# Linear attention followed by a feed-forward layer: loads in batch order with waits between, a second pair of batches worked batch by batch, and a re-tuned order

## The chip, the cores and the metric

The kernel runs on one core of a Trainium2 chip. The metric is the device time of one execution in microseconds (us), smaller is better. Before the change the median of three runs was 384.72 us (383.87 to 385.67). All runs compared below are fast runs, that is, runs not disturbed by the slower state that some executions show.

The engines are called by their names in the profile: PE is TensorE (PEld its weight loads), DVE is VectorE, ACT is ScalarE, POOL is GpSimd, SP is SyncE. SyncE computes nothing; it issues transfers, and its records in the timeline carry the name SPq.

## The reference

There are 8 batches, 8 heads, 576 tokens, a head size of 64 and 128 features. Attention is linear, and its result is the input of a layer norm and a feed-forward layer of 512 to 2048 to 512 columns.

```python
def phi(x):
    proj = np.einsum('bhsd,df->bhsf', x, w_phi)
    proj = proj - np.max(np.abs(proj), axis=-1, keepdims=True)
    return np.concatenate([np.exp(proj), np.exp(-proj)], axis=-1)
q_p, k_p = (phi(q), phi(k))
kv = np.einsum('bhsf,bhsd->bhfd', k_p, v)
z = np.sum(k_p, axis=2)
num = np.einsum('bhsf,bhfd->bhsd', q_p, kv)
den = np.einsum('bhsf,bhf->bhs', q_p, z)[..., None] + 1e-06
attn = num / den                       # then heads side by side: x, (8, 576, 512)
# feed-forward
xn = (x - mu) / np.sqrt(var + 1e-06) * g_ln
out = x + np.maximum(xn @ w_ch1, 0.0) @ w_ch2
```

## The kernel before

The work is cut into 32 units. A unit is two heads: in the first pair of batches two heads of the same batch, in the later pairs one head of each of the two batches. A unit passes through all engines. TensorE transposes q and k (units 0 to 7; from unit 8 on transposing transfers do it), projects them (`pk`, `pq`, `pt`), and makes kv (`n_bank`) and the numerators (`num`). VectorE takes maxima, ScalarE exponentials, GpSimd scales v (`vv`) and writes the tokens (`x`).

When all eight heads of a batch are done, its tokens are complete. Then feed-forward blocks can run: `hT` (input times w1) and `ch` (times w2). Until the first of them, fillers, which are products of zeros (`wz`), are there to keep TensorE's clock up.

A small list scheduler decides the order of the instructions at build time. It plays the program through with estimated durations; on each engine it takes the ready operation with the smallest rank. The rank is the latest start plus a tuned offset, `OFF`, by stage and table. The order it finds is then fixed: on the chip every engine works through its own line in order.

```python
BLOCKS = (((0, 2), (2, 4), (4, 6), (6, 9)), *(((0, 3), (3, 6), (6, 9)),) * (NPAIR - 1))
...
def heads(pair, i, half):
    if pair == 0:                       # first pair: batch by batch
        return i // 4, 2 * (i % 4) + half, 2
    return 2 * pair + half, i, 1        # later pairs: one head of both batches
...
def stage_table(n):                     # three tables of offsets for 32 units
    return (n >= H // 2) + (n >= H)
...
for i in range(EXB):
    ex = consts.tile([P, 2, 2 * P], BF16, name=f"ex{i}")
    nc.gpsimd.memset(ex, 0.0)           # five of them, on GpSimd
...
load_weights()
for n in range(NW):
    load_w1(n, -5 + n, [("came", "q", 1)])
for key in "kqv":
    load_tails(key, 4, next(rank), "SP")
for n in (4, 5):
    for key in "kvq":
        load_main(key, n, 1, next(rank), "SP")
for n in range(NW):
    load_w2(n, rk("w2", 0))             # w2 waits only for w1
```

Of the kernel before, what the change touches and what calls it, by code (L numbers as in the profile page):

```python
# [17 lines left out]
def bcast(ap: bass.AP, dim: int, n: int) -> bass.AP:  # L18
# [9 lines left out]
OFF = (  # L28
    {
        "en": 0, "gln": 404.4, "k": 731.6, "k.copy": 69.4, "k.em": -232.2, "k.exp": 2503.5,  # L30
        "k.max": 95, "k.trans": 40.9, "kv": 899.6, "kv.copy": -103, "ln": 482.7, "mixed": 18.6,
        "mixed.exp": -123.6, "mixed.max": 174.2, "num0": -2477.8, "num0.dve": -58.1,
        "num0.put": 178.6, "num1": 209.2, "num1.dve": 318.7, "num1.put": -457.6, "q.copy": -276.1,
        "q.trans": -426.8, "q0": -1263.9, "q0.em": 149.7, "q0.max": 0, "q1": -821.5,
        "q1.em": -990.6, "q1.max": -13.6, "tails0": -719.9, "tails0.exp": -90.7, "tails1": -225.7,
        "tails1.exp": 0, "vv": 215.8, "w2": 3061.6, "x.copy": -132.9, "x.trans": -1573.1,
    },
    {
        "en": 1225.8, "k": -596.1, "k.copy": 123.9, "k.em": 639.7, "k.exp": 9.2, "k.max": 81.3,
        "k.trans": -90.1, "kv": 0, "kv.copy": -360, "ln": 262.7, "load": 0, "mixed": -1206,  # L40
        "mixed.exp": -223.1, "mixed.max": 1308.1, "num0": 517.5, "num0.dve": -73.3,
        "num0.put": 141.8, "num1": 67.4, "num1.dve": -802.1, "num1.put": 0, "q.copy": -784.4,
        "q.em": 5.6, "q.max": 36.6, "q.trans": 753.5, "qt": -360.9, "rstd": -179.5,
        "tails.exp": 199, "vv": 2452.3, "x.copy": 195.6, "x.trans": -942.9,
    },
    {
        "en": 167.8, "k": 108.9, "k.em": 424.2, "k.exp": -788, "k.max": 25.2, "kv": -30.9,
        "kv.copy": 8.3, "ln": 12.2, "load": 1357.4, "mixed": -2096, "mixed.exp": 54.6,
        "mixed.max": 4.8, "num0": -162.6, "num0.dve": -161.9, "num0.put": -15.2, "num1": -692.4,
        "num1.dve": -457.5, "num1.put": -223.9, "q.em": -210.7, "q.max": -16.1, "qt": -860.5,  # L50
        "rstd": 81.2, "tails.exp": -53.9, "trans": 253.4, "vv": 2822.4, "w1": 1149.9,
    },
)
# [9 lines left out]
class Order:  # L63

    ENGINES = ("PE", "DVE", "ACT", "POOL", "SP")
    START, LAND, RING, TURN, COLD = 1.15, 0.75, 60.0, 0.095, 5.5
# [36 lines left out]
    def run(self):  # L103
# [21 lines left out]
        while True:  # L125
# [30 lines left out]
            for engine in self.ENGINES:  # L156
# [4 lines left out]
                while queue:  # L161
                    item = heapq.heappop(queue)
                    op = item[2]
                    if op.engine:
                        op = None
                        continue
                    full = op.dma and out.get(op.dma[0], 0.0) > self.RING
                    if not full and all(room[res] >= n for res, n in op.acquire):
                        break
                    passed.append(item)  # L170
                    op = None
                for item in passed:
                    heapq.heappush(queue, item)
# [13 lines left out]
                if engine == "PE":  # L187
                    us += self.TURN * (op.mode != mode) + us * (now < self.COLD)
                    mode = op.mode
                elif engine == "DVE" and op.port:  # L190
                    us += min(max(free["POOL"] - now, 0.0), 1.0)
# [7 lines left out]
                if op.dma:  # L199
                    out[op.dma[0]] = out.get(op.dma[0], 0.0) + op.dma[1]  # L200
                    push(now + self.START, 3, op)
# [12 lines left out]
def kernel(  # L214
# [44 lines left out]
    EARLY, NUMB, TILED = 4, 0, 4  # L259
# [13 lines left out]

    wphi_f = consts.tile([P, F], FP32, name="wphi_f")
# [12 lines left out]
    for i in range(2):  # L287
        rows = slice(i * D, (i + 1) * D)
        nc.vector.tensor_copy(out=wbk[rows, i, :], in_=wphi_f[rows, :])
# [24 lines left out]
    for i in range(EXB):  # L314
        ex = consts.tile([P, 2, 2 * P], BF16, name=f"ex{i}")
        nc.gpsimd.memset(ex, 0.0)
        ex_bufs.append(ex)

    w1_sb = consts.tile([P, KC, DH], BF16, name="w1")
    w2_sb = consts.tile([P, JC, DM], BF16, name="w2")  # L320

# [9 lines left out]
    nc.vector.tensor_copy(out=wst, in_=wphi_f)  # L331
# [30 lines left out]
    def issue(queue, rank, dst, src, keys, nbytes, row=1024):  # L362
        eng = nc.sync if queue == "SP" else nc.scalar
        dma(
            queue, rank, nbytes / row, lambda: eng.dma_start(out=dst, in_=src), w=keys,
            us=0.65 if row == 256 else 0.52, ns=0.019 if row == 256 else 0.045,
        )

    def heads(pair, i, half):

        if pair == 0:
            return i // 4, 2 * (i % 4) + half, 2
        return 2 * pair + half, i, 1

    def load_main(key, n, nu, rank, queue):
# [7 lines left out]
        if pair == 0:  # L383
# [9 lines left out]
                262144 * nu,  # L393
            )
            return
        for half in range(2):
# [7 lines left out]
                [(key + str(half), g % NBUF, u) for u in us], 131072 * nu,  # L404
            )

    def load_tails(key, n, rank, queue):
# [4 lines left out]
        for half in range(2):  # L412
# [9 lines left out]
            issue(queue, rank, dst, src, [(key + "x" + str(half), j)], 16384 * TG, row=256)  # L422
# [25 lines left out]
    def load_w2(n, V):  # L448
# [9 lines left out]
        dma("POOL", V, 512, emit, r=[("w1 came", NW - 1)], w=[("w2", n)], us=0.75, ns=0.094)  # L458

    def scale_w1(n, rank):  # L460
# [5 lines left out]
        def scale(kc):  # L466
            nc.vector.tensor_scalar(
                out=w1_sb[:, kc, sl], in0=w1_sb[:, kc, sl], scalar1=gln_sb[:, kc : kc + 1],
                scalar2=-1.0, op0=ALU.mult, op1=ALU.mult,
            )  # L470

        for kc in range(KC):
            add("DVE", 0.3, rank, lambda kc=kc: scale(kc), r=["gln"], w=[("w1", n, kc)])
# [63 lines left out]
    def a_trans_dma(u):  # L537
# [28 lines left out]
        def turn():  # L566
# [6 lines left out]
        add(("DVE", "ACT", "POOL"), (0.12, 0.19, 0.8), rank, cast_mixed,  # L573
# [5 lines left out]
            us=1.3, ns=0.019)  # L579

    def a_mixed(u):
# [11 lines left out]
        def maxima():  # L593
            nc.vector.reduce_max(
                out=u["m"][:, :, u["mx"]],
# [28 lines left out]
    def a_k(u):  # L624
# [17 lines left out]
        def em():  # L642
            t_ = u["em", 1]
            e = u["mx"] + 1
# [7 lines left out]
        def en():  # L652
            e = u["mx"] + 1
            nc.scalar.activation(u["en"][:, 0:e], u["m"][:, 1, 0:e], AF.Exp, scale=-1.0)

        def scale_main(t):
            vb, vx = v_bufs[u["g"] % NBUF], vx_bufs[n // TG % 2]
# [5 lines left out]
            )  # L663
            nc.gpsimd.tensor_copy(  # L664
# [5 lines left out]
                in1=bcast(bcast(e[:, u["mx"] : u["mx"] + 1], 1, 2), 3, D1), op=ALU.mult,  # L670
# [14 lines left out]
        for t, e in ((1, ("em", 1, n % NEM)), (0, ("en", n % NEM))):  # L685
            add("POOL", 1.5, rk("vv", n), lambda t=t: scale_main(t),
                r=[e, *vdata] + [("vv", 1, n % VVB)] * (1 - t), w=[("vv", t, n % VVB)])

    def q_part(u, s):

        qT = u["qkT"][:, 0:512]
        if s is None:
            return qT.rearrange("p (c t) -> p c t", t=P)
        return qT.rearrange("p (h s t) -> p s h t", h=2, s=2)[:, s]

    def a_q(u, s=None):

        n = u["n"]
        x = "" if s is None else str(s)
        nc_ = 4 if s is None else 2  # L700

        def products():
            shape = [P, 2 * nc_, F]
            pool, tag = (ps_A, "A") if s is None else (ps_B, "B")
            u["pq", s] = ps = pool.tile(shape, FP32, tag=tag, name="pq")
            chunks = q_part(u, s)
            for c in range(nc_):
# [4 lines left out]
        def maxima():  # L712
            m, ps = u["m"][:, 0, :], u["pq", s]
            if s is not None:
                out = m[:, 6 * s : 6 * s + 4]
            elif u["pair"]:
                out = m[:, 0:MX]
            else:
                out = m.rearrange("p (s r) -> p s r", s=2)[:, :, 0:4].rearrange(
                    "p s (h a) -> p h s a", h=2  # L720
                )
                ps = ps.rearrange("p (h s a) f -> p h s a f", h=2, s=2)
            nc.vector.reduce_max(out=out, in_=ps, axis=AX.X, apply_absolute_value=True)

        def em():
            lo, hi = {None: (0, u["mx"] + 1), 0: (0, 4), 1: (6, u["mx"] + 1)}[s]
# [4 lines left out]
        parts = (0, 1) if s is None else (s,)  # L731
        room = [("A" if s is None else "B", 1)]
        mk = [("m", 0, p, n % NEM) for p in parts]
        add("PE", mm(nc_, 256), rk("q" + x, n), products, r=[("qkT", n % QB, 0), ("T", n % QB, 0)],
            w=[("pq", s, n)], acquire=room)
        add("DVE", 1.14 if s is None else 0.61, rk(f"q{x}.max", n), maxima, r=[("pq", s, n)],
            w=mk, release=room)
        add("ACT", 0.1, rk(f"q{x}.em", n), em,
            r=mk + [("mx", n % NEM)] * (s != 0), w=[("em", 0, p, n % NEM) for p in parts])

    def a_tails(u, s=None):

        n = u["n"]
        x = "" if s is None else str(s)
        half = 512 if s is None else 256

        def products():
            pool, tag = (ps_A, "A") if s is None else (ps_B, "B")
            u["pt", s] = ps = pool.tile([P, 2 * half], FP32, tag=tag, name="pt")
            for i in range(2):  # L750
                nc.tensor.matmul(
                    ps[:, i * half : (i + 1) * half], wbk[:, i, :], q_part(u, s),
# [3 lines left out]
        def exps(t):  # L756
            out, in_ = u["EA"][:, t, :], u["pt", s]
            if s is not None:
                out = out.rearrange("p (a h s t) -> p s a h t", a=2, h=2, s=2)[:, s]
                in_ = in_.rearrange("p (a h t) -> p a h t", a=2, h=2)  # L760
            nc.scalar.activation(out, in_, AF.Exp, scale=(1.0, -1.0)[t])

        parts = (0, 1) if s is None else (s,)
        room = [("A" if s is None else "B", 1)]
        keys = [[("EA", t, p, n % EAB) for p in parts] for t in range(2)]
        add("PE", mm(2, half), rk("tails" + x, n), products,
            r=[("qkT", n % QB, 0), ("T", n % QB, 0)], w=[("pt", s, n), *keys[0], *keys[1]],
            acquire=room)
# [616 lines left out]
```

## Time and profile before

| | |
|---|---|
| run time, median | 384.72 us |
| span of the profiled execution | 381.3 us |
| time that TensorE needs for all its streamed columns | 320.3 us |
| lost, the difference to the span | 61 us |
| first feed-forward product | 46.3 us |

The third and fourth rows rest on two durations of the trace: eight products of 384 columns take 1.30 us, six of 512 columns 1.29 us, so a column costs 0.42 ns. From the same figures comes a curve. **Lost time** at a moment is that moment minus the columns streamed by then times the cost of a column; what was streamed is found by counting the recorded weight loads, of which none is missing (3562 before, 3542 after), against the built order. Products on 64 rows run two at a time (eight of 128 columns in 0.24 us at 186 us) and count half. The 768,768 columns so counted make 320.3 us at 0.4167 ns each; at 0.42 ns the level at the end would be 2.6 us lower.

The head of the page of the kernel before: busy time by engine, then tenths of busy time in 40 equal slices, the granted TensorE clock and the share of the DMA engines.

```profile
span 381.3 us, 9349 instructions
PE 361.3 (95%) x3562; PEld 230.4 (60%) x3562; DVE 296.8 (78%) x633; ACT 226.3 (59%) x539; POOL 181.5 (48%) x334
...
PE   7999689996997999999999999999999999999995
...
PEclk9999999998999999999999999999999999999999
DMA  7999799799899865967362456210000530110012
```

The 95% of TensorE says little, since fillers and short products with gaps count as busy. The slices say more: 6 and 8 in the fifth and sixth, 6 in the tenth, 7 in the thirteenth, and full from there to the last.

The same kernel by stretches of time. The columns are the length, busy time of each engine with its instructions, the granted clock, the DMA share and GB/s.

```profile
core 0: us, PE busy (x) PEld busy (x) DVE busy (x) ACT busy (x) POOL busy (x), PEclk, DMA share, GB/s
40.00:60.00 20.00, 15.77 (x210) 12.04 (x204) 19.42 (x51) 18.66 (x46) 16.83 (x38) 1.00 0.98 191
80.00:90.00 10.00, 6.52 (x75) 4.05 (x73) 6.28 (x17) 6.47 (x17) 4.87 (x10) 0.97 1.17 225
90.00:100.00 10.00, 10.00 (x108) 6.59 (x107) 8.64 (x20) 8.62 (x23) 6.12 (x10) 0.86 1.06 261
180.00:280.00 100.00, 100.00 (x993) 60.05 (x992) 85.46 (x174) 73.27 (x168) 55.16 (x95) 1.00 0.33 80
```

From 180 us on TensorE is full. What can be won lies before. At 80 to 90 us all four engines drop together while the DMA engines are at 1.17, and the clock dips afterwards. The waits of that stretch (engine and line, what it waited for, total, times, longest) and the line of SyncE in it show how:

```profile
ACT b L547 <- DMA qkT<-b: 3.5, 1, 3.5
PE ch_ps L1150 <- ACT xT L1009: 3.5, 1, 3.5
```

```profile
75.94 1.12 SPq L365 DMA_DIRECT2D v<-in_v_dram  x2
77.11 0.98 SPq L365 DMA_DIRECT2D qk<-in_k_dram  x2
78.13 0.98 SPq L365 DMA_DIRECT2D qk<-in_q_dram  x2
79.16 1.23 SPq L365 DMA_DIRECT2D v<-in_v_dram  x2
80.49 5.68 SPq L568 DMA_TRANSPOSE qkT<-b  x2
```

Eight loads of 256 KB go out ahead of two transposing transfers. ScalarE must wait for those before it may overwrite the buffer `b`; behind that cast, in its line, stands the copy `xT` that TensorE needs.

The start, from VectorE's timeline: the two w_phi casts of the first line take 0.87 us each while GpSimd runs its memsets. The first maxima of k come at 6.74 us.

```profile
3.71 1.76 DVE L289 CAST wbk<-wphi_f 64x128 bf16<-64x128 f32 x2 [2.45 <-DMA wphi_f<-in_w_phi_dram]
...
6.74 1.22 DVE L638 TENSOR_REDUCE m<-pk 128x8 f32<-128x1024 f32 x1 [0.70 <-PE pk L632]
```

### The profile page before, as it was taken

How to read it: one execution, taken by the hardware profiler on the slowest of the kernel's cores; microseconds unless marked ns; L12 is line 12 of the kernel's file. 1: busy time of each engine (PE TensorE's matmuls, PEld its weight loads, DVE VectorE, ACT ScalarE, POOL GpSimd, SP SyncE). 2: the span in 40 equal slices, each digit the busy share in tenths (PEclk: the TensorE clock that was granted, in tenths of full speed). 3: DMA queues.
4: the chain of work that ended last, by engine and by line, in shares of the span. 5: the costliest groups of instructions: out<-in, count | busy, mean ns of one | idle time of the engine just before them, and what ended most of it. 6: DMA issues, size and time to landing. Idle time of an engine off the chain costs nothing.

```text
span 381.3 us, 9349 instructions
## 1 busy us (share of the span) xinstructions
PE 361.3 (95%) x3562; PEld 230.4 (60%) x3562; DVE 296.8 (78%) x633; ACT 226.3 (59%) x539; POOL 181.5 (48%) x334
## 2 busy tenths in 40 slices
PE   7999689996997999999999999999999999999995
PEld 6899567664774555655566656566565555555544
DVE  5689999994999999978988899788879745454532
ACT  3889897776986777877787777867644300000000
POOL 4948968975678756165655851744451000000000
PEclk9999999998999999999999999999999999999999
DMA  7999799799899865967362456210000530110012
GB/s 204 262 234 335 151 258 174 194 243 236 243 259 265 231 184 127 260 114 215 78 148 53 121 119 158 66 28 30 29 29 28 112 93 31 30 55 29 38 45 85
DMA packets 92589, 53.31 MB, mean 140 GB/s; under 512 B 59008, under 2 KB 88064, under 8 KB 92544
## 3 DMA queue, kind: packets, MB, share of 16 engines
q1 hardware_dynamic: 86944, 48.18, 49.0%
q0 software_dynamic: 4224, 4.19, 6.8%
q8 instruction: 28, 0.46, 0.5%
q10 hardware_dynamic: 1376, 0.33, 0.4%
q14 instruction: 17, 0.14, 0.1%
HBM read 36.77 MB, written 9.44 MB: 121 GB/s over the span
## 4 chain that ended last, share of the span: by engine, by line
PE 54%; POOL 1%; DMA 1%; DVE 0%; SPq 0%; issue 0%; DVEq 0%
PE ch_ps L1150 23%; PE hT_ps L1120 22%; PE n_bank L843 2%; PE num L887 1%; PE pk L632 1%; PE pq L784 1%; PE pt L789 1%; DMA out_dram<-o 1%; PE n_bank L838 1%; PE n_bank L887 1%; POOL vv L659 1%; PE n_bank L893 0%; PE n_bank L590 0%; DVE o L1157 0%; POOL vv L668 0%; POOL vv L664 0%
## 5 line engine op out<-in xcount | busy, mean ns | idle before, releaser
L1150 PE MATMUL ch_ps<-w,hT 128*128 128x512 bf16 (+1 forms) x592 | 153.3, 375 | 3.5 <-ACT xT L1009 3.5
L1120 PE MATMUL hT_ps<-xT,w 128*128 128x384 bf16 (+1 forms) x832 | 153.9, 315 | 0.8 <-ACT xT L1009 0.3
L1120 PEld LDWEIGHTS <-w 128*128 128x128 bf16 x832 | 77.6, 98 | 54.0 <-issue 4.6
L1128 DVE TENSOR_SCALAR hT<-hT_ps 128x384 bf16<-128x384 f32 (+1 forms) x136 | 71.3, 525 | 49.4 <-PE hT_ps L1120 47.5
L1150 PEld LDWEIGHTS <-hT 128*128 128x128 bf16 x592 | 54.7, 98 | 44.3 <-issue 5.1
L659 POOL TENSOR_TENSOR vv<-v,em 128x512 bf16<-128x512 f32 x64 | 67.1, 1049 | 23.7 <-ACT em L645 14.9
L917 POOL TENSOR_TENSOR x<-numc,rden 128x384 bf16<-128x384 f32 (+3 forms) x88 | 45.8, 534 | 66.0 <-DVE rden L911 64.0
L1130 ACT ACTIVATE hT<-hT_ps 128x384 bf16<-128x384 f32 (+1 forms) x72 | 33.3, 465 | 66.9 <-PE hT_ps L1120 66.5
L648 ACT ACTIVATE eb<-pk 128x1024 bf16<-128x1024 f32 x64 | 65.7, 1043 | 5.4 <-DVE m L638 5.3
L810 ACT ACTIVATE ea<-pt 128x1024 bf16<-128x1024 f32 x56 | 57.0, 1028 | 15.9 <-PE pt L789 15.4
L638 DVE TENSOR_REDUCE m<-pk 128x8 f32<-128x1024 f32 x32 | 38.8, 1213 | 5.0 <-PE pk L632 4.9
L803 DVE TENSOR_REDUCE m<-pq 128x8 f32<-128x1024 f32 x28 | 33.9, 1210 | 1.0 <-PE pq L784 1.0
L1157 DVE SCALAR_TENSOR_TENSOR o<-ch_ps,rstd,x 128x512 f32<-128x512 f32 (+1 forms) x37 | 26.9, 728 | 9.1 <-PE ch_ps L1150 8.1
L887 PEld LDWEIGHTS <-ea 128*128 128x128 bf16 x512 | 25.2, 98 | 7.7 <-issue 1.7
L843 PE MATMUL n_bank<-vv,eb 128*128 128x65 bf16 x512 | 26.9, 194 | 0.0
L843 PEld LDWEIGHTS <-eb 128*128 128x128 bf16 x512 | 22.3, 98 | 7.0 <-issue 4.1
L668 POOL TENSOR_TENSOR vv<-vx,em 128x130 bf16<-128x130 f32 x64 | 26.0, 406 | 0.0
L549 POOL TENSOR_TENSOR b<-qk,one 128x1024 bf16<-128x1024 f32 x11 | 21.3, 1932 | 9.0 <-DMA qkT<-b 9.0
L1034 DVE BATCH_NORM_STATS2 st<-x 128x6 f32<-128x512 bf16 (+1 forms) x44 | 24.5, 581 | 0.8 <-POOL x L917 0.4
L632 PE MATMUL pk<-wbk,qkT 128*128 128x256 bf16 x128 | 19.2, 272 | 5.5 <-DVE m L803 4.0
L1347 PE MATMUL n_bank<-wz 128*128 128x120 bf16 x309 | 23.0, 223 | 0.4 <-DVE KV L850 0.4
L902 DVE TENSOR_TENSOR numc<-num,em 128x390 f32<-128x390 f32 (+2 forms) x40 | 20.5, 514 | 1.4 <-PE qxT_ps L493 0.7
(89 smaller groups left out, 442.8 us busy)
## 6 DMA issues: line engine op xcount, KB each, us to landing
qk<-in_k_dram SPq DMA_DIRECT2D x32, 256.0 KB, 3.9
v<-in_v_dram SPq DMA_DIRECT2D x32, 256.0 KB, 3.7
qk<-in_q_dram SPq DMA_DIRECT2D x32, 256.0 KB, 4.9
out_dram<-o SPq DMA_DIRECT2D x31, 256.0 KB, 2.6
w<-in_moe_w_ch_dram POOLq DMA_DIRECT2D x8, 512.0 KB, 9.3
out_dram<-o SPq DMA_DIRECT2D x9, 128.0 KB, 2.4
qx<-in_k_dram SPq DMA_DIRECT2D x16, 64.0 KB, 3.9
vx<-in_v_dram SPq DMA_DIRECT2D x16, 64.0 KB, 3.6
```

Source lines behind the costliest of these rows:

```text
L638: nc.vector.reduce_max(out=u["m"][:, 1, 0:MX], in_=u["pk"], axis=AX.X, apply_absolute_value=True)
L648: nc.scalar.activation(u["EB"][:, t, 0:MX, :], u["pk"], AF.Exp, scale=(1.0, -1.0)[t])
L659: nc.gpsimd.tensor_tensor(out=u["vv"][:, t, 0:MX, 0:D], in0=vb[:, hh, :].rearrange("p (c d) -> p c d", d=D), in1=bcast(e[:, 0:MX], 2, D), ...
L803: nc.vector.reduce_max(out=out, in_=ps, axis=AX.X, apply_absolute_value=True)
L810: nc.scalar.activation(u["EA"][:, t, :], u["pt", None], AF.Exp, scale=(1.0, -1.0)[t])
L843: nc.tensor.matmul(ps[:, t, c // 4, :], EB[:, t, c, :], vv[:, t, c, :], start=False, stop=(t == 0 and c == MX - 1), skip_group_check=True,)
L887: nc.tensor.matmul(ps[t][:, i, :], ea(u, t, c), KV[:, t, c // 4, :], start=True, stop=True,)
L917: nc.gpsimd.tensor_tensor(out=dst, in0=st["numc"][ps_, i : i + n, 0:D], in1=bcast(st["rden"][ps_, i : i + n], 2, D), op=ALU.mult,)
L1120: nc.tensor.matmul(st["ps"], w1_sb[:, kc, jj * P : (jj + 1) * P], xT_bufs[xj][:, kc : nt * KC : KC, :], start=(kc == 0), stop=(kc == KC - 1),)
L1128: nc.vector.tensor_relu(h_sb[:, 0 : nt * P], st["ps"])
L1130: nc.scalar.activation(h_sb[:, 0 : nt * P], st["ps"], AF.Relu)
L1150: nc.tensor.matmul(ch[t, c][:, cols], hT[jj][:, rt * P : (rt + 1) * P], w2_sb[:, jj, cols], start=(jj == 0), stop=(jj == JC - 1),)
```

## The change

The intent is fourfold: make feed-forward work available earlier (the first batch before the second, and a second pair that is worked batch by batch too); give loads a fixed order so that they do not crowd out what is needed sooner; free the start from the clash of memsets and casts; and tune the order anew, with fifteen tables of offsets in place of three.

```diff
-    EARLY, NUMB, TILED = 4, 0, 4
+    EARLY, SPLIT, GATE = 4, 2, 0
...
     def heads(pair, i, half):
-        if pair == 0:
-            return i // 4, 2 * (i % 4) + half, 2
+        if pair < SPLIT:
+            return 2 * pair + i // 4, 2 * (i % 4) + half, 2
...
     def stage_table(n):
-        return (n >= H // 2) + (n >= H)
+        return n if n < 12 else 11 + n // 8
...                                       # OFF: 3 tables replaced by 15, all values new
-        nc.gpsimd.memset(ex, 0.0)
+        nc.vector.memset(ex, 0.0)
...
+    def gate(key, n):                     # a tiny transfer that waits for a weight
+        src = w1_sb[0:1, 0, n * WC : n * WC + 8] if key == "w1" else w2_sb[0:1, n * JC // NW, 0:8]
+        add(
+            "SP", 0.6, rk("load", 0), lambda: nc.sync.dma_start(out=seen, in_=src),
+            r=[("w1", n, 0) if key == "w1" else ("w2", n)], w=[("gate", key)], lag=0.0,
+        )
...
+    for key in "kqv":
+        load_tails(key, 4, next(order), "SP")
     load_weights()
     for n in range(NW):
         load_w1(n, -5 + n, [("came", "q", 1)])
+    gate("w1", 1)                         # then the loads of batch 1
...
+        if n == EARLY:
+            for j in range(NW):
+                load_w2(j, rk("w2", 0), [("x", 0, 3, 6), ("came", "q", 6)])
+            gate("w2", GATE)              # then the loads of batch 2
...
-    START, LAND, RING, TURN, COLD = 1.15, 0.75, 60.0, 0.095, 5.5
+    START, LAND, RING, TURN, COLD = 1.15, 0.75, 128.0, 0.095, 5.5
```

Further, the filler tile's memset and the w_phi casts become part of the order (`features()`), the numerators of the first four units are cut otherwise, part of the w1 scaling may go to ScalarE, v is scaled in two operations, the loads of the second pair are 512 KB each, and the scheduler reckons transposing transfers at 1.6 us, not 1.3.

## The prediction

> **What bounds it now.** TensorE: its work, plus the time in which it has none. In the chain of waits eight 384-column products take 1.30 us and six 512-column ones 1.29 us, so a column costs 0.42 ns. All real TensorE instructions of the built order stream 320 us at that rate, before and after the change. The span is 381.3 us, so 61 us are lost. Its timeline against the built order shows where: 28 us before the first feed-forward product (hT) at 46.3 us, while 310 fillers run; 11 us at 66-99 us; 7 us at 99-142 us; 9 us spread over 142-290 us; 6 us at the end. The stretch table has TensorE 100% busy from 180 us.
>
> The loss at 66-99 us is a load stall: at 80-90 us TensorE, VectorE, ScalarE and GpSimd all fall to 49-65% while the DMA share is 1.17, after SyncE issued eight 256 KB loads ahead of two transposing DMAs; the granted clock then dips to 0.86. The loss at 99-142 us is missing feed-forward work: the second pair gives no finished token tile until all 8 units are done (141.7 us), with VectorE 94-100% busy.
>
> **What the change does.**
> 1. The second pair runs batch by batch too: its first tiles are complete after unit 11, not 15, and its first feed-forward block stands at 90 us of streamed columns in the built order, not 106. Cost: smaller, more statistics and output multiplies, about 6 us of GpSimd, off the critical path (GpSimd is 48% busy).
> 2. Batch 0's units are finished before batch 1's: the first hT stands at 14.6 us of columns and 279 fillers, not 18.0 and 310. In the new order ScalarE has about 26 us of work before it, from about 6 us on; before, exponentials of units 4 and 5 came first too. I put it at 38 us.
> 3. Loads in order, w1 alone after batch 0, w2 before batch 2. The gates may delay unit 4, but w2 is first used near 50 us and batch 2's data near 58 us. Most of the stall should go.
> 4. Five GpSimd memsets (0.53 us each) move to VectorE, ahead of w_phi's arrival. Two w_phi casts now take 0.87 us each beside these memsets, the larger third one 0.23 us. The Trainium skill, "SBUF — State Buffer", section "SBUF: two separate sides", says that VectorE and GpSimd take a shared port as an exclusive lock; the trace agrees. Expect about 1 us.
>
> **Sum.** 320 columns + 23 before the first hT (38 - 14.6; was 28) + 7 starvation to the end of pair 1 (was 18) + 9 spread + 6 end = 365 us of span; runs are 3 us longer: **368 us, 361 to 377**. VectorE's durations up to pair 1's first block sum to 100 us, plus 10 idle, against 116 on TensorE, so VectorE only narrowly does not starve it. Chances: faster by over 2% 0.86, within 2% 0.12, slower 0.02.
>
> **Signs.** Right: first hT at 36-41 us; no common dip at 80-90 us and no clock dip; TensorE 95% or more busy at 60-140 us; w_phi casts near 0.3 us. Wrong: hT after 43 us; VectorE or ScalarE waiting for a gated load at 25-60 us; TensorE idle at 120-200 us, the unsplit third pair coming with less backlog.
>
> **What would make it wrong.** The gates make units 4 to 9 late; transposing DMAs queue behind larger loads (512 KB each); ScalarE and VectorE bind the start.

## More of the kernel before

All but two of the q, k and v loads, all but one of the stores, the transposing transfers and a small transfer `x<-xs` (it moves the last 64 tokens of a batch to their partitions) are issued by SyncE, in one line. w1 and w2 are issued by GpSimd.

Lost time is not all waiting. From 180 to 280 us, where TensorE is full, the curve still rises by 5.6 us, since some 1000 products there take on average about 5.6 ns more than their columns.

## The result, and the profile after

The changed kernel took **375.54 us** in the median of four runs (374.89 to 376.10), beside 384.31 us before on the same chip. The ratio is 0.9765, with a 95% interval of 0.9735 to 0.9796. (Ratios here are the mean time of one kernel's fast runs over that of the other's of the same rounds, so not quite the ratio of the medians.) It is faster, inside the range of the forecast, but the gain is 8.8 us where about 17 were forecast.

The page of the changed kernel, same lines as before:

```profile
span 373.7 us, 9269 instructions
PE 356.8 (95%) x3499; PEld 230.7 (62%) x3542; DVE 294.7 (79%) x637; ACT 233.1 (62%) x550; POOL 180.9 (48%) x359
...
PE   6999999997999898999999999999999999999995
...
PEclk9999999999999999999999999999999999999999
DMA  7999499998698798696942729500000082010102
```

The hole in the fifth slice of PE is gone, and so is the one in the thirteenth. The one in the tenth is not (7), and the fourteenth and sixteenth now show 8. In the DMA row a new hole stands in the fifth slice (4). By stretches:

```profile
40.00:60.00 20.00, 19.58 (x257) 15.44 (x257) 18.64 (x43) 17.46 (x42) 16.44 (x36) 1.00 1.00 190
80.00:90.00 10.00, 8.13 (x121) 6.65 (x121) 7.50 (x17) 7.72 (x20) 4.00 (x8) 1.00 0.81 232
90.00:100.00 10.00, 8.93 (x75) 6.46 (x76) 9.02 (x22) 7.55 (x22) 6.76 (x15) 0.83 0.73 198
```

At 80 to 90 us all engines still drop together, and the clock still dips, with the DMA share now at 0.81. It is another stall at the same place. Its waits, and SyncE's line:

```profile
PE hT_ps L1252 <- DVE o L1289: 2.7, 1, 2.7
...
DVE st L1166 <- DMA x<-xs: 1.4, 1, 1.4
...
DVE o L1289 <- DMA out_dram<-o: 1.0, 1, 1.0
```

```profile
78.55 1.06 SPq L497 DMA_DIRECT2D qk<-in_k_dram  x2
79.65 1.35 SPq L497 DMA_DIRECT2D qk<-in_q_dram  x2
81.37 2.41 SPq L497 DMA_DIRECT2D qx<-in_k_dram  x2
83.83 1.28 SPq L497 DMA_DIRECT2D qx<-in_q_dram  x2
85.21 0.62 SPq L1108 DMA_DIRECT2D x<-xs  x1
85.93 1.43 SPq L1214 DMA_DIRECT2D out_dram<-o  x1
```

Before, eight loads stood ahead of two transposing transfers. Now eight stand ahead of the transfer `x<-xs` and the stores. VectorE waits first for the one, then for the other (a store has to free a buffer of `o`), and TensorE waits for VectorE. The dip of the clock agrees in size with the Trainium skill, "TensorE: Matmul & The Clock Gate", section "What's actually happening", which has only full and half speed, switched by windows of about 3.4 us. (From 92 to 95 us the trace has it at 0.50.) At half speed, 0.83 over 10 us means 3.4 us, and before, 0.97 and 0.86 over 10 us each mean 3.4 us as well. That costs TensorE 1.7 us of streaming each time, an estimate from these shares. The dip does not come in every execution: the control below, the same kernel, waits 1.3 us at 87 us and has no dip there, but one of the same length at 120 us, after a wait of 2.0 us. The run with the gates off waits 2.6 us at 88 us and has none.

The first feed-forward product, in TensorE's timeline before and after:

```profile
46.33 1.03 PE L1120 MATMUL hT_ps<-xT,w 128*128 128x256 bf16 x8 [0.31 <-ACT xT L1009]
```

```profile
37.96 0.60 PE L1252 MATMUL hT_ps<-xT,w 128*128 128x256 bf16 x4
```

The start, on VectorE, after the change:

```profile
4.04 0.23 DVE L1375 CAST wbk<-wphi_f 64x128 bf16<-64x128 f32 x1
4.28 0.23 DVE L1376 CAST wst<-wphi_f 128x128 bf16<-128x128 f32 x1
...
8.22 1.22 DVE L786 TENSOR_REDUCE m<-pk 128x8 f32<-128x1024 f32 x1 [0.63 <-PE pk L780]
```

The casts fell to 0.22 us, but the first maxima came 1.5 us later (8.22 against 6.74 us): the new order on TensorE has the transposes of the tails of q and k first, and it waited 1.9 us for the q tails there.

Lost time on the curve, in us (the last column is the span minus 320.3 us):

| | at 40 | 50 | 70 | 100 | 140 | 165 | end |
|---|---|---|---|---|---|---|---|
| before | 24.6 | 29.7 | 32.4 | 39.5 | 46.5 | 48.2 | 61.0 |
| after | 24.0 | 25.7 | 27.1 | 33.3 | 37.6 | 40.2 | 53.4 |
| won | 0.6 | 4.0 | 5.3 | 6.2 | 8.9 | 8.0 | 7.6 |

Most of the gain, 5.3 us, is there at 70 us. From 70 to 100 us the kernel before lost 7.1 us and the changed one 6.2; from 100 to 165 us 8.7 and 6.9; after 165 us 12.8 and 13.2. Each column is one execution, and the control below shows how far two executions of one kernel differ.

### The profile page after: what moved, and what is told of

The parts are those of the page before. It is cut to its first block, busy times and chain, and to the rows that moved or that the text cites. A ratio compares the mean times of both kernels' runs of the same rounds, so it can differ in the third digit from the quotient of the medians.

```text
span 373.7 us, 9269 instructions
## 1 busy us (share of the span) xinstructions
PE 356.8 (95%) x3499; PEld 230.7 (62%) x3542; DVE 294.7 (79%) x637; ACT 233.1 (62%) x550; POOL 180.9 (48%) x359
## 5 line engine op out<-in xcount | busy, mean ns | idle before, releaser
L1282 PE MATMUL ch_ps<-w,hT 128*128 128x512 bf16 (+1 forms) x549 | 141.4, 373 | 3.9 <-DVE hT L1260 1.9
L1260 DVE TENSOR_SCALAR hT<-hT_ps 128x384 bf16<-128x384 f32 (+1 forms) x127 | 67.1, 530 | 38.4 <-PE hT_ps L1252 36.0
L1048 POOL TENSOR_TENSOR x<-numc,rden 128x192 bf16<-128x192 f32 (+4 forms) x112 | 50.1, 464 | 68.9 <-DVE rden L1042 66.6
L807 POOL TENSOR_TENSOR vv<-v,em 128x512 bf16<-128x512 f32 x64 | 68.2, 1067 | 21.4 <-ACT em L793 11.3
L1262 ACT ACTIVATE hT<-hT_ps 128x384 bf16<-128x384 f32 (+1 forms) x81 | 37.3, 463 | 63.3 <-PE hT_ps L1252 62.9
L796 ACT ACTIVATE eb<-pk 128x1024 bf16<-128x1024 f32 x64 | 64.4, 1029 | 4.2 <-DVE m L786 3.5
L1166 DVE BATCH_NORM_STATS2 st<-x 128x6 f32<-128x256 bf16 (+1 forms) x52 | 25.3, 513 | 2.3 <-DMA x<-xs 1.4
L819 POOL TENSOR_TENSOR vv<-vx,em 128x130 bf16<-128x130 f32 x64 | 25.7, 401 | 0.0
L1190 ACT ACTIVATE xc<-x,mv 128x512 bf16<-128x512 bf16 x22 | 15.5, 730 | 7.5 <-DVE mv L1181 4.7
L1033 DVE TENSOR_TENSOR numc<-num,em 128x390 f32<-128x390 f32 (+2 forms) x36 | 19.1, 531 | 0.9 <-PE num L1025 0.4
```

The costliest lines, as they stand in the source:

```text
L796: nc.scalar.activation(u["EB"][:, t, 0:MX, :], u["pk"], AF.Exp, scale=(1.0, -1.0)[t])
L807: nc.gpsimd.tensor_tensor(out=u["vv"][:, t, 0:MX, 0:D], in0=vb[:, hh, :].rearrange("p (c d) -> p c d", d=D), in1=bcast(e[:, 0:MX], 2, D), ...
L1048: nc.gpsimd.tensor_tensor(out=dst, in0=st["numc"][ps_, at, 0:D], in1=bcast(st["rden"][ps_, at], 2, D), op=ALU.mult,)
L1260: nc.vector.tensor_relu(h_sb[:, 0 : nt * P], st["ps"])
L1262: nc.scalar.activation(h_sb[:, 0 : nt * P], st["ps"], AF.Relu)
L1282: nc.tensor.matmul(ch[t, c][:, cols], hT[jj][:, rt * P : (rt + 1) * P], w2_sb[:, jj, cols], start=(jj == 0), stop=(jj == JC - 1),)
```

## The experiments

Twelve kernels were run: the changed kernel unedited, nine with one edit each, and two with two edits (the old offsets with one pair, and the last). All gave the right result, except that two compute a wrong one, as said there. Ratios are to the kernel before of the same rounds. The theories were these: (1) the gates delay what comes behind them; (2) the clash on the port between VectorE and GpSimd takes the rest; (3) the feed-forward work now starts early enough, but VectorE, or ScalarE, cannot deliver the units as fast; (4) the loads on SyncE's line are late or crowd out others; (5) no single one: behind each limit the next stands close.

**Control.** The changed kernel again, unedited.

> The changed kernel itself, as a control on the same chip as the next three: ratio to the kernel before 0.977, as measured first (0.974 to 0.980).

It took 373.83 us, ratio 0.9776 (0.9737 to 0.9815), span 371.7 us. Two executions of the same kernel differ by up to 4 us on the curve (29.7 us at 100 us here, 33.3 there), which sets the scale for what follows.

**Gates off.** The two tiny transfers are not emitted; the planned order is kept.

```diff
-            "SP", 0.6, rk("load", 0), lambda: nc.sync.dma_start(out=seen, in_=src),
+            "SP", 0.6, rk("load", 0), None,
```

> The changed kernel with the order of every engine kept, but the two tiny gate transfers not issued, so batch 1's loads follow batch 0's at once and share the DMA engines with w1, and batch 2's with w2. Theory A (the ordering of loads is worth something): w1 lands some us later than 28 us and the first feed-forward product moves from 38 us to 40 us or later, time up by 1 to 4 us (377 to 380). Theory B (the gates only delay batch 1's loads and SyncE's line, and the loads were never the limit at the start): same time or faster by 1 to 2 us (373.5 to 375.5).

It took 374.61 us, ratio 0.9765 (0.9721 to 0.9808). Without the gates the weights took longer to land (the two weights together 11.3 us in the median, against 9.3), but the first feed-forward product came at 37.7 us all the same. The gates cost nothing, and no run shows that they earn anything. Theory 1 falls.

**Memsets back on GpSimd.**

```diff
-        nc.vector.memset(ex, 0.0)
+        nc.gpsimd.memset(ex, 0.0)
```

> The changed kernel with the five ex memsets back on GpSimd, all orders kept. The w_phi casts should go from 0.22 us back to 0.8 to 0.9 us each (port lock). If the start hangs on the casts, the first products and the whole run come 1 us later (376.5). If TensorE's wait for the tails of q at 5 to 7 us hides it, the time stays at 375.5 within 0.5 us.

It took 374.08 us, ratio 0.9745 (0.9703 to 0.9786). VectorE's timeline has the slow casts back, 1.61 us for two:

```profile
3.86 1.61 DVE L1375 CAST wbk<-wphi_f 64x128 bf16<-64x128 f32 x2 [2.60 <-DMA wphi_f<-in_w_phi_dram]
```

So the memsets do slow the casts, and this is worth nothing in the total: after the casts TensorE still waits for the tails of q (1.1 us in this run, which got to the first maxima at 7.54 us). The cost was real, and hidden.

**Small casts on ScalarE.** At 119 to 122 us VectorE's subtraction of the mean (`xc`) takes 3.59 us for two, while GpSimd scales v; alone one takes 0.34 us. The two timelines of the changed kernel:

```profile
118.69 3.59 DVE L1185 TENSOR_SCALAR xc<-x,mv 128x512 bf16<-128x512 bf16 x2
```

```profile
119.17 2.04 POOL L807 TENSOR_TENSOR vv<-v,em 128x512 bf16<-128x512 f32 x2
```

The four small casts by VectorE (`b` from `qx`), which take 1.38 us each in the mean and up to 1.57 us, were given to ScalarE.

```diff
-                engine, b16[:, MX * P :].rearrange("p (i d) -> p i d", i=2),
+                "ACT" if engine == "DVE" else engine, b16[:, MX * P :].rearrange("p (i d) -> p i d", i=2),
```

> The changed kernel, orders kept, with the four 128x128 fp32-to-bf16 casts that VectorE took (1.375 us mean, waiting for the port that GpSimd holds) issued on ScalarE instead (0.3 us). Theory A (VectorE's waits for the port starve TensorE between 100 and 165 us): VectorE loses 5.5 us of busy time, time down by 1.5 to 4 us (371.5 to 374). Theory B (VectorE is not what TensorE waits for there): within 0.7 us of 375.5.

It took 373.18 us, ratio 0.972 (0.9678 to 0.9763). At 100 to 120 us TensorE was full in the profiled execution, but lost time at 140 us was 37.5 us against 36.2 in the control (that execution, at 376.14 us, was the slowest of its six). The time lies in what the expectation asked for if the port starves TensorE (371.5 to 374), but so does that of the unedited control, 373.83 us. Some 2 us by the ratios, not separated from the control. The clash is seen; theory 2 as the cause of the missing 8 us is not.

**One pair batch by batch**, with the order planned anew.

```diff
-    EARLY, SPLIT, GATE = 4, 2, 0
+    EARLY, SPLIT, GATE = 4, 1, 0
```

> The changed kernel with only the first pair batch by batch, as before the change (SPLIT 1 for 2); the scheduler orders anew with the same offsets. Theory A (the prediction: batch by batch for the second pair removes the lack of feed-forward work from 99 to 142 us): time up by 4 to 8 us, 379 to 384, TensorE idle between 100 and 160 us. Theory B (the lost time there comes from SyncE's line and VectorE's port waits, not from missing work): within 2 us of 375.5.

It took 404.05 us, ratio 1.0524 (1.0478 to 1.057). It keeps up until 130 us (lost time 36.2 us, 37.2 in the changed kernel) and then breaks down (40.3 at 140 us, 67.9 at 180 us). TensorE is busy only half of the time there, and the clock is at half speed:

```profile
140.00:160.00 20.00, 10.28 (x110) 7.22 (x110) 12.90 (x28) 10.15 (x31) 9.88 (x17) 0.50 0.58 139
```

But the offsets had been tuned for two pairs, so this run confounds the split with the tuning. Hence the next two.

**The offsets of before, with two pairs and with one.** The three old tables are mapped to the fifteen.

```diff
+OFF = {}
+for _n in range(32):
+    _t = _n if _n < 12 else 11 + _n // 8
+    for _k, _v in OFF_BEFORE[(_n >= 4) + (_n >= 8)].items():
+        OFF.setdefault(_k, {})[_t] = _v
```

> The changed kernel's code with the three old tables of priority offsets in place of the per-unit ones; the scheduler orders anew. If the new order of instructions, not the loads or the split, carries the gain, this loses all of it or more: 384 us or slower. If the split and the loads carry it, it keeps most: 376 to 380 us.

> As the run with the old offsets, but with the second pair in the old form too (SPLIT 1). The difference of the two is the worth of batch by batch for the second pair under offsets tuned for the old form. Theory A of the prediction: the split is worth 4 us or more even so, this is 4 us slower than the run with SPLIT 2. Theory B: it is worth nothing without an order that uses it, equal within 2 us or this one faster.

Two pairs took 404.86 us, ratio 1.0572 (1.0538 to 1.0607); one pair, 414.65 us, ratio 1.0828 (1.0785 to 1.0871). So the split is worth about 10 us under the old offsets and about 30 us under the new ones (404.05 against 374). Neither pair of numbers is its worth in the change: each part is good only with an order tuned for it. With the old offsets the change is 21 us slower than the kernel before. The split, the fifteen tables and the other edits can't be told apart by taking one away.

**Half of the maxima.** VectorE's maxima of units 8 to 15 run over half of the features. The result is wrong.

```diff
-                out=u["m"][:, 1, 0:MX], in_=u["pk"], axis=AX.X, apply_absolute_value=True
+                out=u["m"][:, 1, 0:MX], in_=u["pk"][:, :, 0 : F // 2] if H <= n < 2 * H else u["pk"],
+                axis=AX.X, apply_absolute_value=True
...                                       # the same for pq
```

> Wrong result on purpose; the changed kernel with all orders kept. For units 8 to 15 the row maxima of k and q read half of the columns, so VectorE has about 0.55 us less work in each of 16 instructions, 9 us between some 75 and 165 us. Theory A (VectorE is what limits the stretch from 70 to 165 us, so TensorE's lost time there cannot be taken away elsewhere): 4 to 9 us faster than the changed kernel, ratio to the kernel before 0.955 to 0.966 for 0.977. Theory B (SyncE's line, the port or TensorE itself limits): within 2 us, 0.972 to 0.98.

It took 374.22 us (three fast runs), ratio 0.9729 (0.9683 to 0.9776). VectorE was busy for 79.9 us between 70 and 165 us in place of 86.6. Lost time was 32.7 us at 100 us and 39.3 at 165, between those of the two executions of the changed kernel.

**Half of the exponentials.** ScalarE's exponentials of units 8 to 15 run over half of the columns, some 13 us of ScalarE less. The result is wrong.

```diff
+            f = F // 2 if H <= n < 2 * H else F
             nc.scalar.activation(
-                u["EB"][:, t, 0:MX, :], u["pk"], AF.Exp, scale=(1.0, -1.0)[t]
+                u["EB"][:, t, 0:MX, 0:f], u["pk"][:, :, 0:f], AF.Exp, scale=(1.0, -1.0)[t]
             )
...                                       # the same for EA
```

> Wrong result on purpose; orders kept. For units 8 to 15 the four large exponentials of each unit cover half of the columns, so ScalarE has about 13 us less work in the same stretch. If VectorE alone limits it: within 2 us of the changed kernel (ratio 0.972 to 0.98). If ScalarE limits as much: 4 us or more faster (0.966 or less). ScalarE is 77 to 99% busy there against 84 to 100% for VectorE, so I expect 1 to 3 us.

It took 374.64 us (three fast runs), ratio 0.9775 (0.9709 to 0.9841); ScalarE was busy for 66.8 us in place of 79.1. With the run before it this speaks against theory 3: less work for VectorE alone or for ScalarE alone did not bring the 4 us or more that the theory asked for. The intervals leave room for 2 to 4 us each, and a run with both at once was not made.

**75 more fillers** ahead of the first feed-forward product, so that it comes 4 us later.

```diff
+        i = next(i for i, op in enumerate(done) if op.emit and op.engine == "PE"
+                 and "first.<locals>" in op.emit.__qualname__)
+        for _ in range(75): ...           # insert a filler at i
```

> Orders kept; 75 more filler products (4.1 us of TensorE) just ahead of the first feed-forward product, which then starts near 42 us in place of 38. Theory A (the prediction's sum: time lost before the first feed-forward product stays lost): 3 to 4 us slower, ratio 0.985 to 0.988. Theory B (the other engines limit the stretch behind it, so TensorE catches up until about 100 us): less than 1.5 us slower, ratio below 0.982.

It took 375.5 us, ratio 0.9788 (0.9754 to 0.9822). The curve is the telling part:

| lost time, us | at 40 | 50 | 70 | 80 | 100 | 120 | 165 |
|---|---|---|---|---|---|---|---|
| control | 22.8 | 24.4 | 25.9 | 26.5 | 29.7 | 33.4 | 38.6 |
| 75 more fillers | 25.5 | 28.0 | 30.1 | 30.3 | 32.3 | 33.9 | 39.2 |

It is four microseconds behind the control at 70 us and within one of it at 120 us (three behind the other execution of the same order at 70 us, one ahead of it at 100 us). From 80 to 120 us the control loses 6.9 us and this kernel 3.6: its stretch of 80 to 90 us has no stall.

```profile
80.00:90.00 10.00, 9.94 (x136) 7.40 (x136) 9.53 (x18) 9.34 (x25) 6.40 (x14) 1.00 0.97 279
```

So in the changed kernel several microseconds of an earlier start are not worth microseconds at the end. What is ready at 100 to 120 us is set elsewhere.

**Loads later.** SyncE's loads after 40 us are moved up to 8 us back in its line, with at least 10 us of planned lead left, so that stores, transposing transfers and `x<-xs` go first.

```diff
+        def at(op):                       # loads on SP only
+            if op.engine == "SP" and op.t0 > 40.0 and op.emit and "issue" in op.emit.__qualname__ and op.users:
+                use = min(o.t0 for o in op.users)
+                return max(op.t0, min(op.t0 + 8.0, use - 10.0))
+            return op.t0
+        done.sort(key=at)
```

> The changed kernel, every other engine's order kept, with SyncE's loads after 40 us moved up to 8 us later in its line (never nearer than 10 us of planned time to their first use), so the move of the mixed tile's rows, the stores and the transposing transfers come ahead of loads that nobody needs yet. Theory A (these wait behind loads on SyncE, and that is the stall at 87 to 92 us, with TensorE idle 2.7 us and the clock at 0.83 after it): the stall and the clock dip go, 3 to 5 us faster than the control. Theory B (TensorE makes up such stalls later, since VectorE limits up to 165 us anyway): within 1 us of the control.

It took 378.73 us, ratio 0.9894 (0.9854 to 0.9933), so it is some 5 us slower than the control. No wait of TensorE over 1 us stands at 80 to 100 us (in the control 1.3 us at 87 us, in the first execution 2.7 us and the dip of the clock), and a new stall stands at 140 to 150 us:

```profile
80.00:90.00 10.00, 9.29 (x142) 7.88 (x142) 9.92 (x24) 9.10 (x24) 4.46 (x10) 1.00 1.12 274
90.00:100.00 10.00, 9.95 (x96) 6.55 (x97) 9.58 (x22) 9.59 (x29) 9.77 (x20) 1.00 0.90 213
140.00:150.00 10.00, 6.81 (x88) 4.40 (x87) 6.27 (x14) 4.70 (x8) 4.17 (x11) 0.96 0.47 113
```

Lost time at 100 us was 29.7 us, the same as in the control. Taking away this stall earned nothing against the control. The new one has the old form: a transposing transfer goes out at 143.5 us behind moved loads (one pair of them takes SyncE 3.15 us), ScalarE's cast `b` waits 5.1 us for it, and TensorE waits 3.0 us for a copy behind that cast. The Trainium skill, "Perfetto Trace Analysis", section "Optimization Strategy", advises to find the gaps on the engine that matters, see what blocks there, and make that start sooner. That was done here, and it was not enough: the gap was one of several that follow closely.

**First loads of batch 2 earlier.** In the control SyncE stands from 32 to 43 us in front of `x<-xs`, whose data is not ready (10.8 us in the view of SyncE's waits), and then in front of the gate. The DMA engines have almost nothing to do meanwhile. The buffers of the next six loads are free by then. They were put ahead, and the gates left out.

```diff
+        sp = [op for op in done if op.emit and op.engine == "SP"]
+        loads = [op for op in sp if "issue" in op.emit.__qualname__]
+        mv = next(i for i, op in enumerate(done) if op.emit and op.engine == "SP" and "move" in op.emit.__qualname__)
+        moved = [op for op in done[mv:] if op in loads][:6]
+        for op in moved:
+            done.remove(op)
+        done[mv:mv] = moved
```

> The changed kernel without the two gates (alone worth nothing: 0.9765), and with the six loads that SyncE issues at 46-50 us (k and q of units 8 and 9 and their tails, some 1.2 MB) put in front of the transfer x<-xs on which SyncE stands until 44 us. Their buffers are free by then. They should issue at about 32-36 us, while the DMA engines are nearly idle (share 0.17 at 35-40 us in the control), and everything behind them on SyncE's line moves up by as much as the buffers allow. No other engine's order changes. Theory C (the arrival of batch 2's data through SyncE's one line and the DMA engines limits 60-120 us): lost time at 100 us falls from 28.7 to 26 or less, ratio 0.970 or less. Rival D (no single limit: behind each stall the next one stands within a microsecond or two, and what is won at one place is lost at the next): lost time differs by no more than 2 us anywhere after 100 us, ratio 0.974 to 0.981. A ratio above 0.985: the early loads hold up something that is needed sooner (w2, or the transposes of units 6 and 7).

It took **372.46 us** (371.09 to 374.44), ratio 0.9692 (0.9666 to 0.9718), the lowest of all. The stretch of 35 to 40 us, in the control and in this kernel:

```profile
35.00:40.00 5.00, 5.00 (x81) 4.79 (x79) 4.99 (x12) 4.26 (x11) 4.58 (x11) 1.00 0.17 58
```

```profile
35.00:40.00 5.00, 5.00 (x93) 4.87 (x91) 4.99 (x15) 4.39 (x12) 4.14 (x10) 1.00 1.10 359
```

The transfer was done in the idle time as intended. SyncE's line then was through with its loads 5 us earlier, and its two transposing transfers took 2 us less (3.48 against 5.68 us). But the casts `b`, which the transposing transfers wait for, ran no earlier, for they have their place in ScalarE's and VectorE's lines. ScalarE's and SyncE's timelines, first both of the control:

```profile
59.12 1.04 ACT L695 CAST b<-qk 128x1024 bf16<-128x1024 f32 x1 [0.36 <-issue]
```

```profile
60.43 0.55 SPq L497 DMA_DIRECT2D v<-in_v_dram  x1
61.16 5.68 SPq L716 DMA_TRANSPOSE qkT<-b  x2
```

and then both of this kernel:

```profile
59.48 1.05 ACT L702 CAST b<-qk 128x1024 bf16<-128x1024 f32 x1
```

```profile
55.26 0.59 SPq L504 DMA_DIRECT2D v<-in_v_dram  x1
61.41 3.48 SPq L723 DMA_TRANSPOSE qkT<-b  x2
```

Five microseconds won on SyncE became a wait of SyncE for ScalarE. The expected sign on the curve, 26 us or less at 100 us, failed: it is 30.8 us there, 38.5 at 165 us, against 29.7 and 38.6 in the control. The time met what theory 4 asked for (0.970 or less), the profile did not. The intervals of this ratio and of the control's, both from the same chip, do not overlap, so a gain of 1.4 us (by medians) to 3.2 us (by ratios) is likely, but its place is not shown: the profiled execution was the slowest of the five, at 374.44 us.

## Why the prediction was right or wrong

**Right: the direction, the range, and the start.** The first feed-forward product was put at 38 us and came at 37.96. The loss before it was put at 23 us and was 23.4 (37.96 minus 14.6 us of columns). That the earlier start is worth its 5 us in the sum is not shown: in the run with more fillers 4 us of it were given back, at a cost of about half a microsecond (0.9788 against 0.9776). So no run says which part of the change earned the 8.8 us.

**Right: the rest behind the end of the second pair.** The prediction had 9 + 6 = 15 us of loss there, unchanged. The curve has 13.2 us after 165 us, 12.8 before.

**Wrong in size: "7 starvation to the end of pair 1 (was 18)".** This is the step that failed, and it alone accounts for the missing half. From the first feed-forward product (23.4) to 165 us (40.2) the changed kernel lost 17 us, not 7; at 151 us, where the last numerators of the second pair are made, it is 16. In sum: 23.4 + 16.8 + 13.2 = 53.4 us, where the prediction had 45. Before, 20 us were lost from the first feed-forward product (28.3) to 165 us (18 of them by 142 us, where the prediction ends that term), so 3 were won. Where the split and the order of the loads were to pay, the gain was 0.9 us (70 to 100 us) and 1.8 us (100 to 165 us), in the control 3.3 us and none.

Of these 17 us TensorE stood idle for 7.3; 1.7 went with the half clock. The rest, some 8 us, is what is lost with TensorE full: at the rate of 180 to 280 us (5.8 us in 100 us after the change) 127 us lose 7.4 us, an estimate. So a term of 7 us for all losses of this stretch had no room for any wait.

The reckoning behind that term compared amounts of work: VectorE's durations up to a certain block against TensorE's. The runs speak against one engine's amount of work as the limit of this stretch: 7 us less of VectorE or 12 us less of ScalarE brought nothing clear of the control. TensorE's idle time is mostly single waits, each through several engines (2.7 us at 88 us, 1.9 us at 121 us).

**Wrong: "Most of the stall should go", no common dip and no dip of the clock at 80 to 90 us.** The transposing transfers were freed, but `x<-xs` and two stores took their place behind the loads. The clock fell to 0.83 against 0.86 in the first execution; in the control it did not fall there but at 120 us. TensorE, put at 95% or more from 60 to 140 us, was at 81% from 80 to 90 us and at 90% from 120 to 140. And where a run removed this stall (loads later), nothing was gained by 100 us.

**Wrong in effect: "about 1 us" from the memsets.** The mechanism held, with casts at 0.22 us instead of 0.87. The run that moved the memsets back (0.8 us each) agrees with the Trainium skill's shared port, cited in the prediction. But the first maxima came later, at 8.22 us, for another reason, and that run was no slower.

**Right: the gates.** They delayed nothing measurable. The 512 KB loads took 6.2 us to land in the median against 4.0 us for 256 KB; no run isolates what this costs.

**What stays open.** What sets the pace from 70 to 165 us is not settled. Not the gates, not the amount of work of VectorE or of ScalarE alone, not TensorE's start, not the stall at 88 us alone; both engines together, and the port beyond the small casts, were not tried. The fillers run and the last run agree with theory 5: each engine's line is fixed, and a gain in one line turns into a wait for the next, since the order was tuned for the old arrival times. That is shown at one place (the casts at 59 us) and argued for the rest. A test would be to plan the whole order anew with the early loads, which needs a new tuning and was not tried.

## What to carry to other kernels

When a kernel's lines are fixed in order, compare the sums of work to find what can bind, but don't forecast a stretch from them: follow the waits through the engines, and ask which wait ends second-last. A stall that is plain in the profile may be worth nothing, so take it away alone before building on it. Look for stretches in which the issuing engine stands in front of one transfer while the DMA engines are idle; loads with free buffers are worth trying ahead of that one.

## What the Trainium skill lacked or had wrong

- "TensorE: Matmul & The Clock Gate", section "What's actually happening", ties the fall to half speed to at least one idle window of about 3.4 us. Here a clock of 0.83 in 90 to 100 us followed a longest wait of TensorE of only 2.7 us, from 88.3 to 91.0 us; in the control one of 2.0 us was enough, and with the gates off one of 2.6 us was not. The length of the throttled time, 3.4 us, agrees.
- "DMA: Bandwidth & Descriptors", section "Issuing engines are not separate DMA queues", says that issuing from several engines only saves the sequencer's time, usually small against the transfer. It does not speak of a transfer that waits for its own data and holds back those behind it: SyncE stood 10.8 us in front of `x<-xs`, with the DMA share at 0.17 for 5 us of it. Whether another issuing engine for it would pay was not run; putting six loads ahead of it took the time from 373.83 to 372.46 us.
- "SBUF — State Buffer", section "Who interferes with whom", agrees with the trace (`xc` 3.59 us for two beside GpSimd's `vv`, 0.34 us alone; casts 0.87 against 0.22 us). What it cannot tell is that neither showed a cost in the total time clear of the control's 373.83 us (374.08 us with the memsets back on GpSimd, 373.18 us with the small casts moved).
